# A gated SSM and MLP mix on one core: first tokens in two halves, PSUM seeds two tiles ahead, last output piece from another queue

## The chip, the cores and the metric

The kernel runs on one core of a Trainium2 chip. The metric is device time in microseconds of one execution. Most executions agree within 0.3%; one early execution of the kernel before took 283.59 us and is left out as not fast.

## The reference

For 2048 tokens of width 640, the result is a gated sum of a diagonal state-space model and a two-layer network. Cut to what matters:

```python
def reference(...):                                     # shortened
    g = sigmoid((x * gate_w).sum(-1, keepdims=True))
    # A: complex diagonal recurrence over the tokens
    Bu = einsum("bld,pd->blp", x, B_bar)                # B_bar, Lam_bar from Lambda, dt
    for t in range(L):
        h = Lam_bar * h + Bu[:, t, :]
    a = 2 * einsum("blp,dp->bld", hseq, Cmat).real + x * Dskip
    # B: two layers
    b = gelu(einsum("bsd,df->bsf", x, w1) + b1)
    b = einsum("bsf,fd->bsd", b, w2) + b2
    return g * a + (1 - g) * b
```

## The kernel before

The tokens go in four chunks of 512 (`CH`), each of four tiles of 128 (`P`). `ff1` is x·w1 with the gelu, `ssm` is x·B with the scan, `fin_b` is gelu·w2, `fin_a` is h·C plus the skip. TensorE does all the products, ScalarE (ACT) evacuates most of PSUM, into whose banks the products are written, and VectorE (DVE) does the complex rotations, the scans, and the last step of the output. In the traces DVE and ScalarE run their instructions in the order in which the program emits them (in the kernel before, DVE's L214, 216, 217, 218, 219, 221, 223 and 225 start in this order between 5.32 and 6.75 us).

The head. The first token chunk comes in two DMAs, then the first part of w1 in five strips (one per 128 rows, seven column tiles wide), all from one queue. TensorE warms up on zeros, transposes the tokens into five PSUM banks (one per 128 features), and starts `ff1`, strip by strip into seven banks:

```python
FA = KF // 2                       # 7 of 14 column tiles of w1 in the first strips
load_xn(0, 2)                      # tokens 0..255, then tokens 256..511
# ... parameters ...
for kd in range(KD):
    nc.sync.dma_start(out=w1a[kd][:], in_=B_w1[kd * P:(kd + 1) * P, 0:cut1])
# ... w1b, B, C, w2 ...
pTs = [bank(BF16) for _ in range(KD)]              # one PSUM bank per feature strip
for kd in range(KD):
    transposes(kd, 0)                              # tokens 0..255
nc.tensor.transpose(pA[:, 0:3 * KS], prmA[:], ident[0:3 * KS, 0:3 * KS])
for kd in range(KD):
    transposes(kd, 1)                              # tokens 256..511
# copies to SBUF: DVE takes strips 0, 2, 4 and ScalarE strips 1, 3
```

The seeds. The skip x·Dskip is not added at the end. DVE writes it into a PSUM bank first (`seed`), and the ten matmuls of `fin_a` accumulate onto it. The seed for a token tile is emitted one tile ahead:

```python
def fin_b(c):
    for a in range(TPC):
        if a == TPC - 1:
            seed(c * TPC)          # tile 0 of fin_a, one tile ahead
        # ... 28 matmuls, evacuated by ScalarE ...
def fin_a(c):
    for a in range(TPC):
        if a < TPC - 1:
            seed(ti + 1)
        # ... 20 matmuls onto the seeds, output step on DVE, DMA out ...
```

The planner. Where seeds, outputs and scan steps stand in DVE's order is decided while the program is built, by a small model of the engines' times. `pe(cols)` adds up TensorE's time from a starting value; a scan step is let out before a seed if the model says that it can start first. This number therefore changes the order of instructions and nothing else:

```python
class Clock:
    pe = 6.6
    act = 13.0
    dve = 0.0
```

## Time and profile before

| | kernel before |
|---|---|
| time, fast runs | 220.7 to 221.4 us |
| span of the profiled run | 219.2 us |
| TensorE, DVE, ScalarE busy | 97%, 86%, 43% |
| first `ff1` matmul (timeline) | 6.20 us |
| first matmul of `ssm(0)`, that is `BT_re` | 21.53 us |
| first matmul of `fin_a(0)`, that is `CT_re` | 73.47 us |
| last matmul starts, span ends | 216.07, 219.19 us |
| TensorE's waits for seeds (start to start) | 1.64 us |

Two lines of the page, the busy time of TensorE and the chain that ended last:

```profile
PE 213.4 (97%) x1276; PEld 125.1 (57%) x1287; DVE 189.3 (86%) x393; ACT 94.6 (43%) x153; POOL 5.0 (2%) x15
...
DVE 74%; PE 19%; issue 3%; DMA 2%; SPq 0%; DVEq 0%
```

TensorE is almost always busy, and yet the chain runs mostly through DVE. The two are as close as that: DVE is idle for only 2.9 us in all from 12.5 to 190 us, so a seed that stands late in DVE's order is late on the chip.

What TensorE waited for (name, then us in total, times, longest; the line of the start, before the first matmul, is left out):

```profile
...
PE bank L508 <- DVE bank L475: 0.7, 2, 0.5
PE bank L278 <- DMA w1a_80<-in_B_w_dram: 0.3, 1, 0.3
```

These totals count idle time from the modelled end of the last matmul, which lies after the moment when TensorE could have taken the next one. It is better to subtract starts. The timeline around 181 us (start, duration, engine, line, operation):

```profile
179.80 1.28 DVE L398 TENSOR_TENSOR_SCAN g<-r_c,carry,v 128x512 bf16<-128x512 f32 x1
180.32 0.84 PE L508 MATMUL bank<-CT_im,hs 128*128 128x320 bf16 x5
...
181.12 0.90 DVE L475 TENSOR_TENSOR bank<-xn,Dbc 128x320 f32<-128x320 bf16 x2
181.66 0.84 PE L508 MATMUL bank<-CT_re,hs 128*128 128x320 bf16 x5 [0.50 <-DVE bank L475]
```

Five matmuls of 320 columns are normally followed by the next five after 0.68 us. Here 181.66 − 180.32 = 1.34 us, so 0.66 us are lost (0.50 by the list of waits), while DVE finishes a scan and then writes the seed (181.12). Five such stretches (0.35 us at 79, 0.27 at 128, 0.18 at 131, 0.66 at 181, 0.18 at 184) add up to 1.64 us.

The head:

```profile
4.16 1.00 PE L197 MATMUL bank<-ident,xn 128*128 128x128 bf16 x10
...
5.21 0.73 PE L197 MATMUL bank<-ident,xn 128*128 128x128 bf16 x10
...
5.53 0.43 DVE L216 COPY xT_76<-bank 128x512 bf16<-128x512 bf16 x1
5.64 0.60 ACT L220 ACTIVATE xT_76<-bank 128x512 bf16<-128x512 bf16 x1
...
6.20 1.68 PE L278 MATMUL bank<-xT_76,w1a_80 128*128 128x512 bf16 x7 [0.25 <-DMA w1a_80<-in_B_w_dram]
...
11.12 0.31 ACT L263 ACTIVATE cq<-absq,halfpi 128x20 f32<-128x20 f32 x1
...
12.82 1.28 ACT L283 ACT_TABLE_LOAD   x1 [1.39 <-DVE colB L306]
...
14.12 1.26 ACT L283 ACTIVATE gel<-bank,colB 128x512 bf16<-128x512 f32 x2
```

The transposes of the second token half (`5.21`) run while TensorE has nothing else to do: the first weight strip lands at 6.15. Between the last of them and the first `ff1` matmul only 0.42 us are lost. DVE and ScalarE copy strips 0 and 1 at the same time (5.53 and 5.64), from two banks. ScalarE is done with the sines at 11.43, and its first gelu comes at 14.12.

The tail, the last five matmuls and the two issues that end the output:

```profile
215.85 0.44 PE L508 MATMUL bank<-CT_im,hs 128*128 128x128 bf16 x5
216.22 0.82 SPq L519 DMA_DIRECT2D out_dram<-ot  x2
```

The second of the two issues starts at 216.71 (the line merges both), 0.03 us after DVE has finished its data at 216.68.

### The profile page before, as it was taken

The page shows a single profiled execution, that of the slowest core. Times are in us where ns is not written, and L with a number is a line of the kernel's source. Part 1 is how long each engine was busy: PE and PEld are TensorE (multiplying, and loading weights), DVE is VectorE, ACT ScalarE, POOL GpSimd, SP SyncE. Part 2 cuts the span into 40 slices and gives each one's busy share as a digit, 9 for nine tenths or more (in the row PEclk, how much of TensorE's full clock was granted, in tenths as well). Part 3 has the DMA queues.
Part 4 walks back from the last instruction along what each step waited for, and adds up shares of the span by engine and source line. Part 5 has one row for each costly group of instructions (what it writes and reads, how often), then busy time and mean ns, then how long its engine had stood idle before and what let it go on. Part 6 is the DMA issues. An engine that isn't in the chain of part 4 may idle for free.

```text
span 219.2 us, 3326 instructions
## 1 busy us (share of the span) xinstructions
PE 213.4 (97%) x1276; PEld 125.1 (57%) x1287; DVE 189.3 (86%) x393; ACT 94.6 (43%) x153; POOL 5.0 (2%) x15
## 2 busy tenths in 40 slices
PE   7999999999999999999999999999999999999994
PEld 3444444444577765444467766444457776777773
DVE  1979999999999999999999999999999999800173
ACT  2779656675688102556652200456673210022100
POOL 6001000000000000000000000000000000000000
PEclk9999999999999999999999999999999999999999
DMA  6999999920000016000000003400000000200011
GB/s 192 355 229 171 224 290 300 197 87 0 0 0 3 0 42 201 0 0 0 0 3 0 0 3 92 147 1 3 0 0 0 3 0 30 71 22 1 0 64 60
DMA packets 31072, 15.31 MB, mean 70 GB/s; under 512 B 23823, under 2 KB 31056, under 8 KB 31056
## 3 DMA queue, kind: packets, MB, share of 16 engines
q1 hardware_dynamic: 30930, 15.09, 27.3%
q8 instruction: 10, 0.16, 0.3%
q14 instruction: 6, 0.05, 0.1%
q0 software_dynamic: 96, 0.00, 0.0%
q10 hardware_dynamic: 30, 0.00, 0.0%
HBM read 7.22 MB, written 2.62 MB: 45 GB/s over the span
## 4 chain that ended last, share of the span: by engine, by line
DVE 74%; PE 19%; issue 3%; DMA 2%; SPq 0%; DVEq 0%
DVE g L398 19%; DVE wb L379 11%; DVE wa L379 10%; PE bank L508 9%; PE bank L489 7%; DVE v L379 7%; DVE hs L379 6%; DVE ot L513 3%; DVE bank L475 3%; PE bank L278 3%; DMA w1a_80<-in_B_w_dram 2%; DVE CT_re L367 2%; DVE CT_im L367 2%; DVE g L329 1%; DVE TSIN L330 1%
## 5 line engine op out<-in xcount | busy, mean ns | idle before, releaser
L489 PE MATMUL bank<-w_sb,gel 128*128 128x320 bf16 x448 | 61.6, 299 | 0.0
L489 PEld LDWEIGHTS <-gel 128*128 128x128 bf16 x448 | 43.7, 98 | 17.7
L283 ACT ACTIVATE gel<-bank,colB 128x512 bf16<-128x512 f32 (+1 forms) x56 | 37.1, 694 | 16.8 <-PE bank L278 16.7
L445 ACT ACTIVATE bu<-bank 128x512 bf16<-128x512 f32 x40 | 23.9, 597 | 40.6 <-PE bank L442 28.6
L508 PEld LDWEIGHTS <-hs 128*128 128x128 bf16 x330 | 31.8, 98 | 13.5 <-issue 1.8
L398 DVE TENSOR_TENSOR_SCAN g<-r_c,carry,v 128x512 bf16<-128x512 f32 x30 | 37.1, 1269 | 0.0
L492 ACT ACTIVATE gb<-bank,gcol 128x320 f32<-128x320 f32 x32 | 16.4, 528 | 46.2 <-PE bank L489 46.2
L508 PE MATMUL bank<-CT_re,hs 128*128 128x320 bf16 (+2 forms) x165 | 27.1, 295 | 0.8 <-DVE bank L475 0.7
L513 DVE SCALAR_TENSOR_TENSOR ot<-bank,gcol,gb 128x320 bf16<-128x320 f32 (+2 forms) x33 | 17.6, 534 | 11.9 <-PE bank L508 11.7
L508 PE MATMUL bank<-CT_im,hs 128*128 128x320 bf16 (+2 forms) x165 | 27.1, 295 | 0.0
L475 DVE TENSOR_TENSOR bank<-xn,Dbc 128x320 f32<-128x320 bf16 (+2 forms) x33 | 14.4, 481 | 6.3 <-ACT gb L492 6.3
L442 PEld LDWEIGHTS <-BT_im 128*128 128x128 bf16 x100 | 9.8, 98 | 11.8
L442 PEld LDWEIGHTS <-BT_re 128*128 128x128 bf16 x100 | 9.8, 98 | 11.5
L379 DVE TENSOR_TENSOR v<-wa,wb 128x512 bf16<-128x512 bf16 x40 | 15.2, 421 | 0.6
L379 DVE TENSOR_TENSOR wa<-TCOS,g 128x1024 bf16<-128x1024 bf16 x20 | 13.7, 685 | 0.1
L379 DVE TENSOR_TENSOR wa<-TCOS,bu 128x1024 bf16<-128x1024 bf16 x20 | 13.7, 684 | 0.0
L379 DVE TENSOR_TENSOR wb<-TSIN,g 128x1024 bf16<-128x1024 bf16 x20 | 13.7, 683 | 0.0
L379 DVE TENSOR_TENSOR wb<-TSIN,bu 128x1024 bf16<-128x1024 bf16 x20 | 13.7, 683 | 0.0
L398 DVE TENSOR_TENSOR_SCAN g<-r_c,v 128x512 bf16<-128x512 f32 x10 | 11.7, 1208 | 0.0
L379 DVE TENSOR_TENSOR hs<-wa,wb 128x512 bf16<-128x512 bf16 x20 | 8.5, 423 | 0.6
L379 DVE TENSOR_TENSOR hs<-wb,wa 128x512 bf16<-128x512 bf16 x20 | 8.4, 418 | 0.0
L442 PE MATMUL bank<-xT_76,BT_im 128*128 128x512 bf16 x25 | 6.2, 379 | 0.0
(157 smaller groups left out, 242.0 us busy)
## 6 DMA issues: line engine op xcount, KB each, us to landing
out_dram<-ot SPq DMA_DIRECT2D x15, 160.0 KB, 1.8
w_sb<-in_B_w_dram SPq DMA_DIRECT2D x1, 2080.0 KB
xn<-in_A_x_dram SPq DMA_DIRECT2D x3, 640.0 KB, 5.1
xn<-in_A_x_dram SPq DMA_DIRECT2D x2, 320.0 KB, 3.4
gz<-zrow SPq DMA_DIRECT2D x16, 0.5 KB, 2.0
w1a_80<-in_B_w_dram SPq DMA_DIRECT2D x1, 224.0 KB, 4.4
w1a_81<-in_B_w_dram SPq DMA_DIRECT2D x1, 224.0 KB
w1a_82<-in_B_w_dram SPq DMA_DIRECT2D x1, 224.0 KB, 4.6
```

The source lines that it names most:

```text
L278: nc.tensor.matmul(p[:m, :], lhsT=w, rhs=xT[c][:, kd, :], start=(kd == 0), stop=(kd == KD - 1))
L283: nc.scalar.activation(out=gel[c][:m, kf, :], in_=p[:m, :], func=ACT.Gelu_apprx_tanh, bias=b1_c[:m, kf:kf + 1])
L367: nc.vector.scalar_tensor_tensor(out=CT[:, ks, :], in0=CT[:, ks, :], scalar=sc[:, ks:ks + 1], in1=t[:], op0=ALU.mult, op1=ALU.add)
L379: nc.vector.tensor_tensor(out=o, in0=a, in1=b, op=op)
L398: nc.vector.tensor_tensor_scan(s["g"][:, ri, :], r_c[:, ks:ks + 1].to_broadcast([P, CH]), s["v"][:, ri, :], init, ALU.mult, ALU.add)
L442: nc.tensor.matmul(p[:], lhsT=BT[:, kd, ks * P:(ks + 1) * P], rhs=xT[c][:, kd, :], start=(kd == 0), stop=(kd == KD - 1))
L445: nc.scalar.activation(out=bu[:, ri, :], in_=p[:], func=ACT.Identity)
L475: dve_now(ck.pe, 0.45, lambda: nc.vector.tensor_tensor(out=p[:, 0:d1 - d0], in0=xn[c][:, a, d0:d1], in1=Dbc[:, d0:d1], op=ALU.mult))
L489: nc.tensor.matmul(p[:, 0:d1 - d0], lhsT=gel[c][:m, kf, lo:lo + P], rhs=w2_sb[:m, kf, d0:d1], start=(kf == 0), stop=(kf == KF - 1))
L492: nc.scalar.activation(out=gb[:, d0:d1], in_=p[:, 0:d1 - d0], func=ACT.Identity, scale=gcol[:, 1, ti:ti + 1])
L508: nc.tensor.matmul(p[:, 0:d1 - d0], lhsT=hs[c][:, j, lo:lo + P], rhs=CT[:, j % KS, d0:d1], start=False, stop=(j == 2 * KS - 1), skip_group ...
L513: nc.vector.scalar_tensor_tensor(out=ot[:, d0:d1], in0=p[:, 0:d1 - d0], scalar=gcol[:, 0, ti:ti + 1], in1=gbs[ti][:, d0:d1], op0=ALU.mult, ...
```

## The change

The intent, in three parts: start `ff1` on the first 256 tokens as soon as their tokens and the first weight strip are there, with the other 256 tokens loaded behind the strips; emit each seed two tiles ahead; and send the last 32 KB of output from ScalarE's queue so that it does not queue behind the piece before. The planner's starting number changes too, from 6.6 to 5.2, as the head is to start earlier. The warm-up on zeros is shortened as well, from seven matmuls of 512 columns to six and two of 128; it belongs to the head. Cut to its core:

```diff
-FA = KF // 2
+FA = 6
-    load_xn(0, 2)
+    load_xn(0, 0, H)
     for kd in range(KD):
         nc.sync.dma_start(out=w1a[kd][:], in_=B_w1[kd * P:(kd + 1) * P, 0:cut1])
+    load_xn(0, H, TPC)
 # ...
-        pe = 6.6
+        pe = 5.2
 # ...
-    pTs = [bank(BF16) for _ in range(KD)]
+    pT = bank(BF16)
+    def strip(kd, h):            # strips 0..3 share one bank, strip 4 lies in pA's
+        return pT[:, kd * HT:(kd + 1) * HT] if kd < 4 else pA[:, (h + 1) * HT:(h + 2) * HT]
+    def take(kd, h):
+        dst = xT[0][:, kd, h * HT:(h + 1) * HT]
+        if kd % 2 == 0:
+            nc.vector.tensor_copy(out=dst, in_=strip(kd, h))
+        else:
+            nc.scalar.activation(out=dst, in_=strip(kd, h), func=ACT.Identity)
 # ... first-half transposes and take(kd, 0), then colA and the first trigonometry steps
+    for kd in range(KD):
+        if kd == KD - 1:
+            transposes(1)
+            for j in range(KD):
+                take(j, 1)
+        for kf in range(FA):
+            ff1_mm(banks[kf], 0, kf, kd, 0, HT)
 # ... the sines; then the same 30 matmuls for the second half, and the gelus
-            if a == TPC - 1:
-                seed(c * TPC)
+            if a >= TPC - 2:
+                seed(c * TPC + a - (TPC - 2))
-            if a < TPC - 1:
-                seed(ti + 1)
+            if a < TPC - 2:
+                seed(ti + 2)
 # ...
-                    nc.sync.dma_start(out=out2d[ti * P:(ti + 1) * P, s0:d1], in_=ot[:, s0:d1])
+                    q = nc.sync if i == 1 else nc.scalar
+                    q.dma_start(out=out2d[ti * P:(ti + 1) * P, s0:d1], in_=ot[:, s0:d1])
```

Below, "the head" is the first part with all that belongs to it, "the seeds" and "the tail" are the other two, and "the planner's number" is the 5.2.

More of the change, by code (lines that the diff above doesn't have):

```diff
@@ L110, with load_xn @@
     H = TPC // 2
-    def load_xn(c, parts=1):
-        xn[c] = xnp.tile([P, TPC, D], BF16, name="xn")
-        n = TPC // parts
-        for h in range(parts):
-            r0 = c * CH + h * n * P
-            nc.sync.dma_start(out=xn[c][:, h * n:(h + 1) * n, :], in_=x2d[r0:r0 + n * P, :].rearrange("(a p) d -> p a d", p=P))
-    load_xn(0, 2)
+    def load_xn(c, a0=0, a1=TPC):
+        if a0 == 0:
+            xn[c] = xnp.tile([P, TPC, D], BF16, name="xn")
+        r0 = c * CH + a0 * P
+        nc.sync.dma_start(out=xn[c][:, a0:a1, :], in_=x2d[r0:r0 + (a1 - a0) * P, :].rearrange("(a p) d -> p a d", p=P))
+    load_xn(0, 0, H)
     nc.scalar.dma_start(out=prmA[0:KS, :], in_=A_log_dt.rearrange("(j p) -> j p", p=P))
@@ L189, with transposes @@
     wps = bank()
-    for _ in range(7):
+    for _ in range(6):
         nc.tensor.matmul(wps[:], lhsT=warm[:, 0:P], rhs=warm[:], start=True, stop=True)
+    for _ in range(2):
+        nc.tensor.matmul(wps[:, 0:P], lhsT=warm[:, 0:P], rhs=warm[:, 0:P], start=True, stop=True)
     pA = bank(BF16)
-    pTs = [bank(BF16) for _ in range(KD)]
-    def transposes(kd, h):
-        for a in range(h * H, (h + 1) * H):
-            nc.tensor.transpose(pTs[kd][:, a * P:(a + 1) * P], xn[0][:, a, kd * P:(kd + 1) * P], ident[:])
-    for kd in range(KD):
-        transposes(kd, 0)
+    pT = bank(BF16)
+    HT = H * P
+    def strip(kd, h):
+        return pT[:, kd * HT:(kd + 1) * HT] if kd < 4 else pA[:, (h + 1) * HT:(h + 2) * HT]
+    def transposes(h):
+        for kd in range(KD):
+            o = strip(kd, h)
+            for a in range(H):
+                nc.tensor.transpose(o[:, a * P:(a + 1) * P], xn[0][:, h * H + a, kd * P:(kd + 1) * P], ident[:])
+    def take(kd, h):
[4 more added lines that the diff above has]
+            nc.scalar.activation(out=dst, in_=strip(kd, h), func=ACT.Identity)
+    transposes(0)
     nc.tensor.transpose(pA[:, 0:3 * KS], prmA[:], ident[0:3 * KS, 0:3 * KS])
-    for kd in range(KD):
-        transposes(kd, 1)
     def col(name, dtype=F32, n=KS):
@@ L213 @@
     r_c = col("r_c")
+    for kd in range(KD):
+        take(kd, 0)
     nc.vector.tensor_copy(out=colA[:], in_=pA[:, 0:3 * KS])
     nc.scalar.activation(out=dt16[:], in_=ldt_c, func=ACT.Exp)
-    nc.vector.tensor_copy(out=xT[0][:, 0, :], in_=pTs[0][:, 0:CH])
     nc.vector.tensor_copy(out=dt32[:], in_=dt16[:])
@@ L219 @@
     nc.vector.tensor_tensor(out=th_c[:], in0=dt32[:], in1=lim_c, op=ALU.mult)
-    nc.scalar.activation(out=xT[0][:, 1, :], in_=pTs[1][:, 0:CH], func=ACT.Identity)
     nc.vector.tensor_scalar(out=thp_c[:], in0=th_c[:], scalar1=INV_2PI, scalar2=None, op0=ALU.mult)
     nc.scalar.activation(out=r_c[:], in_=dtl[:], func=ACT.Exp)
-    nc.vector.tensor_copy(out=xT[0][:, 2, :], in_=pTs[2][:, 0:CH])
-    nc.scalar.activation(out=xT[0][:, 3, :], in_=pTs[3][:, 0:CH], func=ACT.Identity)
-    nc.vector.tensor_copy(out=xT[0][:, 4, :], in_=pTs[4][:, 0:CH])
     scr = gelp.tile([P, KF * CH // 2], F32, name="gel")
@@ L253, with ff1_mm, ff1_act, ff1 @@
     nc.vector.tensor_tensor(out=red, in0=u, in1=kk[:], op=ALU.subtract)
+    sth, cth = sq[:, 0:KS], cq[:, 0:KS]
+    sL, cL = sq[:, KS:2 * KS], cq[:, KS:2 * KS]
+    sH, cH = sq[:, 2 * KS:3 * KS], cq[:, 2 * KS:3 * KS]
+    sQ, cQ = sq[:, 3 * KS:4 * KS], cq[:, 3 * KS:4 * KS]
+    hs = [None] * NCH
+    gel = [None] * NCH
+    gbs = [None] * NT
+    sizes = [P] * (KF - 1) + [F_LAST + 1]
+    def ff1_mm(p, c, kf, kd, t0=0, t1=CH):
+        m = sizes[kf]
+        w = w1a[kd][:, kf * P:kf * P + m] if kf < FA else w1b[kd][:, (kf - FA) * P:(kf - FA) * P + m]
+        nc.tensor.matmul(p[:m, t0:t1], lhsT=w, rhs=xT[c][:, kd, t0:t1], start=(kd == 0), stop=(kd == KD - 1))
+        pe(t1 - t0)
+    def ff1_act(p, c, kf):
+        m = min(sizes[kf], F - kf * P)
+        nc.scalar.activation(out=gel[c][:m, kf, :], in_=p[:m, :], func=ACT.Gelu_apprx_tanh, bias=b1_c[:m, kf:kf + 1])
+        act(0.69)
+        if kf == KF - 1:
+            nc.scalar.activation(out=zrow[F_LAST:F_LAST + 1, :], in_=p[F_LAST:F_LAST + 1, :], func=ACT.Tanh, scale=0.5)
+            act(0.6)
+            for a in range(TPC):
+                ti = c * TPC + a
+                nc.sync.dma_start(out=gz[:, ti:ti + 1], in_=zrow[F_LAST:F_LAST + 1, a * P:(a + 1) * P])
+    def ff1(c, k0=0):
+        for kf in range(k0, KF):
+            p = bank()
+            for kd in range(KD):
+                ff1_mm(p, c, kf, kd)
+            ff1_act(p, c, kf)
+            let_out(ck.pe)
+    def gel_tile(c):
+        gel[c] = gelp.tile([P, KF, CH], BF16, name="gel")
+        nc.gpsimd.memset(gel[c][F_LAST:F_LAST + 1, KF - 1, :], 1.0)
+    gel_tile(0)
+    banks = [bank() for _ in range(FA)]
+    for kd in range(KD):
+        if kd == KD - 1:
[4 more added lines that the diff above has]
+            ff1_mm(banks[kf], 0, kf, kd, 0, HT)
     nc.scalar.activation(out=FS[:, :, 0:HC], in_=red, func=ACT.Sin, scale=TWO_PI_M)
@@ L263 @@
     nc.scalar.activation(out=cq[:], in_=absq[:], func=ACT.Sin, scale=-TWO_PI_M, bias=halfpi[:])
-    sth, cth = sq[:, 0:KS], cq[:, 0:KS]
-    sL, cL = sq[:, KS:2 * KS], cq[:, KS:2 * KS]
-    sH, cH = sq[:, 2 * KS:3 * KS], cq[:, 2 * KS:3 * KS]
-    sQ, cQ = sq[:, 3 * KS:4 * KS], cq[:, 3 * KS:4 * KS]
-    hs = [None] * NCH
-    gel = [None] * NCH
-    gbs = [None] * NT
-    sizes = [P] * (KF - 1) + [F_LAST + 1]
-    def ff1_mm(p, c, kf, kd):
-        m = sizes[kf]
-        w = w1a[kd][:, kf * P:kf * P + m] if kf < FA else w1b[kd][:, (kf - FA) * P:(kf - FA) * P + m]
-        nc.tensor.matmul(p[:m, :], lhsT=w, rhs=xT[c][:, kd, :], start=(kd == 0), stop=(kd == KD - 1))
-        pe(CH)
@@ L281, in ff1_act @@
-    def ff1_act(p, c, kf):
-        m = min(sizes[kf], F - kf * P)
-        nc.scalar.activation(out=gel[c][:m, kf, :], in_=p[:m, :], func=ACT.Gelu_apprx_tanh, bias=b1_c[:m, kf:kf + 1])
-        act(0.69)
-        if kf == KF - 1:
-            nc.scalar.activation(out=zrow[F_LAST:F_LAST + 1, :], in_=p[F_LAST:F_LAST + 1, :], func=ACT.Tanh, scale=0.5)
-            act(0.6)
-            for a in range(TPC):
-                ti = c * TPC + a
-                nc.sync.dma_start(out=gz[:, ti:ti + 1], in_=zrow[F_LAST:F_LAST + 1, a * P:(a + 1) * P])
@@ L292, in ff1 @@
-    def ff1(c):
-        gel[c] = gelp.tile([P, KF, CH], BF16, name="gel")
-        nc.gpsimd.memset(gel[c][F_LAST:F_LAST + 1, KF - 1, :], 1.0)
-        groups = [range(0, FA)] if c == 0 else []
-        groups += [[kf] for kf in range(FA if c == 0 else 0, KF)]
-        for kfs in groups:
-            banks = {}
-            for kd in range(KD):
-                for kf in kfs:
-                    if kd == 0:
-                        banks[kf] = bank()
-                    ff1_mm(banks[kf], c, kf, kd)
-                if c == 0 and kfs[0] == 0 and kd == 3:
-                    nc.tensor.transpose(pA[:, P:P + NB], prmB[:], ident[0:NB, 0:NB])
-                    nc.vector.tensor_copy(out=colB[:], in_=pA[:, P:P + NB])
-                    for j in range(KD):
-                        nc.vector.tensor_copy(out=w1b[j][:, n1b - 1:n1b], in_=pA[:, P + j:P + j + 1])
-            for kf in kfs:
-                ff1_act(banks[kf], c, kf)
-            let_out(ck.pe)
@@ L313 @@
-    ff1(0)
+    for kd in range(KD):
+        for kf in range(FA):
+            ff1_mm(banks[kf], 0, kf, kd, HT, CH)
+        if kd == 2:
+            nc.tensor.transpose(pA[:, P:P + NB], prmB[:], ident[0:NB, 0:NB])
+            nc.vector.tensor_copy(out=colB[:], in_=pA[:, P:P + NB])
+            for j in range(KD):
+                nc.vector.tensor_copy(out=w1b[j][:, n1b - 1:n1b], in_=pA[:, P + j:P + j + 1])
+    for kf in range(FA):
+        ff1_act(banks[kf], 0, kf)
+    ff1(0, FA)
     lo, hi = slice(0, HC), slice(HC, HB)
@@ L523 @@
     ssm(0)
+    gel_tile(1)
     ff1(1)
@@ L533 @@
     ssm(2)
+    gel_tile(2)
     ff1(2)
@@ L539 @@
     ssm(3)
+    gel_tile(3)
     ff1(3)
```

## The prediction

> **What bounds it now.** The page gives TensorE 213.4 of 219.2 us (97%) at full granted clock. From its first FF1 matmul (6.20 us, timeline) to the last one (216.3) it issues matmul after matmul: 216 ns per 512 columns, 136 ns per 320. DVE is busy 86% and has almost no idle from 12.5 to 190 us, so it is the near-critical second engine; the chain of waits running through DVE (74%) reflects that it is always late, not that TensorE starves: the list of waits charges DVE with only 0.7 us of TensorE idle. Start-to-start distances say more: five stretched steps in the output matmuls (L508), all waiting for a PSUM skip seed (L475): 0.35 us at 79, 0.27 at 128, 0.18 at 131, 0.66 at 181, 0.18 at 184: 1.64 us. The head costs 6.2 us: transposes 4.16 to 5.9, then about 0.3 us for the first weight strip, landed at 6.15 (DMA issues). The tail after the last matmul is 2.9 us.
>
> **What changes.**
> 1. Seeds two tiles ahead. No work added (16 tiles either way). In the new DVE order each seed stands one tile earlier. Walking that order with the trace's durations (seed pair 0.80 us, scan 1.19, wide product 0.60, output 0.45 us of DVE time) every seed is done 2 us or more before its matmul; hs of chunk 0 moves behind four seeds, to about 72.5, needed after 73.7. Gain: nearly all of 1.64 us, on the critical path since TensorE is dense elsewhere.
> 2. Head. The DMA engines are full from 2.5 us (350 to 400 GB/s by windows). The first strip now has 328+197 KB in front of and in it, before 655+229: 360 KB less at about 350 GB/s, so landing at 5.1 instead of 6.15. First half transposes end about 5.1. So FF1 starts near 5.2 instead of 6.2. But ten second-half transposes, formerly run inside that wait, now stand in the FF1 stream: 10 x 58 ns = 0.58 us. The second token half, now queued behind five strips, lands near 8.0 (estimate from w1a_84's 8.47 and 163 KB less); TensorE reaches it at 5.2 + 4 x 6 x 109 ns = 7.8: 0.1 to 0.3 us of new wait. Thirty extra matmuls cost 30 x 2.5 ns = 0.08 us (the Trainium skill, "TensorE: Matmul & The Clock Gate", "Wait — 56ns, not 53.3ns?", gives N/2.4 GHz + 2.5 ns; the trace's 216 ns at 512 agrees). Net gain about 0.3 us, not 1. The trigonometry on DVE starts about 0.6 us earlier (12.3 instead of 12.98), more slack for everything on DVE.
> 3. Last piece from ScalarE's queue. The SyncE queue issued it at 216.71, 0.03 us after its data (216.68): nothing to win. The Trainium skill, "DMA: Bandwidth & Descriptors", "Issuing engines are not separate DMA queues", says a second issuer saves only issue time. 0 +- 0.15 us.
>
> **Time.** Fast runs of before: 220.8 to 221.3, profile 221.0. Minus 1.6, minus 0.3: 219.1 to 219.2 us, 0.8% less: inside 2%. Range 218.3 to 220.4. Faster by over 2%: 2%; within: 97%; slower: 1%.
>
> **What the profile would show.** No TensorE wait for DVE seeds in L529 (step 1 right). First FF1 matmul 5.1 to 5.4, the w1a_0 landing about 5.1; a TensorE gap of 0.1 to 0.3 us before the second transposes; first BT_re matmul at 21.2 instead of 21.53 (step 2 right). The distance from last matmul to end still 2.8 to 3.0 us (step 3).
>
> **What would make it wrong.** The second token half landing after 8.5 us, which eats the head's gain; DVE reaching the second half's copies late, behind the trigonometry (about 8.6, needed 9.3); seeds that wait for a PSUM bank and stall DVE in order; output evictions late enough to hold banks from the next matmuls.

## The result and the profile after

The changed kernel took 220.37 us (median of 6 runs, 219.99 to 220.39) against 221.23 us (median of the five fast runs). A ratio here is the mean time of one kernel's fast runs over that of the other's of the same rounds, so not quite the ratio of the medians. It is 0.9965, with a 95% interval from 0.995 to 0.998: 0.35% or 0.8 us less, where 0.8% or 1.9 us had been predicted.

| | before | after | predicted |
|---|---|---|---|
| first `ff1` matmul | 6.20 | 5.39 | 5.1 to 5.4 |
| first `w1` strip landed | 6.15 | 4.42 | 5.1 |
| second token half landed | 4.79 | 8.33 | 8.0 |
| first gelu | 14.12 | 15.29 | not given |
| first matmul of `ssm(0)` | 21.53 | 22.50 | 21.2 |
| first of `fin_a(0)` to last matmul | 142.60 | 140.98 | about 141.0 (142.60 less 1.6) |
| last matmul's start to end of span | 3.12 | 3.17 | unchanged |
| waits for seeds | 1.64 | 0 | nearly 0 |

The stages from 73 us on did what was predicted; the head went 0.97 us the wrong way. The same lines of the page:

```profile
PE 213.6 (98%) x1318; PEld 128.3 (59%) x1318; DVE 189.7 (87%) x396; ACT 94.6 (43%) x155; POOL 4.9 (2%) x15
...
PE 93%; ACT 3%; DVE 2%; issue 0%
```

The chain no longer runs through DVE. TensorE's waits, again without the start:

```profile
...
PE bank L278 <- ACT gel L283: 0.4, 1, 0.4
PE bank L206 <- DMA xn<-in_A_x_dram: 0.2, 1, 0.2
PE bank L278 <- DVE xT_76 L211: 0.2, 1, 0.2
```

No seed is left in this list, and three waits of the head have come. Around 181 us:

```profile
176.78 0.88 DVE L496 TENSOR_TENSOR bank<-xn,Dbc 128x320 f32<-128x320 bf16 x2
...
179.70 0.90 DVE L496 TENSOR_TENSOR bank<-xn,Dbc 128x320 f32<-128x320 bf16 x2
...
180.50 0.84 PE L529 MATMUL bank<-CT_im,hs 128*128 128x320 bf16 x5
...
181.18 0.84 PE L529 MATMUL bank<-CT_re,hs 128*128 128x320 bf16 x5
```

The starts of TensorE stand 0.68 us apart. The seed of the tile that waited before, the second of `fin_a(2)`, is written at 176.78 and done 3.5 us before its first matmul (181.18); what DVE writes at 179.70 is the seed of the third tile. The head:

```profile
5.05 0.29 DVE L211 COPY xT_76<-bank 128x256 bf16<-128x256 bf16 x1 [3.51 <-PE bank L206]
...
5.37 0.39 ACT L213 ACTIVATE xT_76<-bank 128x256 bf16<-128x256 bf16 x1 [2.09 <-DVE xT_76 L211]
5.39 0.82 PE L278 MATMUL bank<-xT_76,w1a_80 128*128 128x256 bf16 x6 [0.16 <-DVE xT_76 L211]
5.79 0.49 DVE L211 COPY xT_76<-bank 128x256 bf16<-128x256 bf16 x2 [0.45 <-ACT xT_76 L213]
...
6.12 0.38 ACT L213 ACTIVATE xT_76<-bank 128x256 bf16<-128x256 bf16 x1 [0.36 <-DVE xT_76 L211]
...
7.35 0.82 PE L278 MATMUL bank<-xT_76,w1a_83 128*128 128x256 bf16 x6
...
8.38 0.73 PE L206 MATMUL bank<-ident,xn 128*128 128x128 bf16 x10 [0.20 <-DMA xn<-in_A_x_dram]
...
8.71 0.83 DVE L263 TENSOR_TENSOR gel<-gel,bu 128x640 f32<-128x640 f32 x1
...
9.45 0.28 DVE L211 COPY xT_76<-bank 128x256 bf16<-128x256 bf16 x1
...
9.79 0.81 PE L278 MATMUL bank<-xT_76,w1a_80 128*128 128x256 bf16 x6
...
10.51 0.38 ACT L213 ACTIVATE xT_76<-bank 128x256 bf16<-128x256 bf16 x1 [0.36 <-DVE xT_76 L211]
...
10.91 1.28 ACT L314 ACT_TABLE_LOAD   x1
...
13.68 0.30 ACT L323 ACTIVATE cq<-absq,halfpi 128x20 f32<-128x20 f32 x1
...
13.99 1.28 ACT L283 ACT_TABLE_LOAD   x1
...
15.22 0.38 PE L278 MATMUL bank<-xT_76,w1b_89 128*128 128x512 bf16 x1
...
16.03 0.38 PE L278 MATMUL bank<-xT_76,w1b_85 128*128 128x512 bf16 x1 [0.42 <-ACT gel L283]
```

Read it in five places. (1) The copies of a half go hand over hand: DVE 5.05, ScalarE 5.37, DVE 5.79, ScalarE 6.12. (2) TensorE comes to the second half at 8.01 us (7.35 plus six steps of 0.109) and takes its first transpose at 8.38. (3) Its last transpose starts at 8.89, but the first copy follows only at 9.45, because DVE is in the third step of the trigonometry (from 8.71). In late_transposes below, where DVE was idle, the first copy starts 0.15 us after the last transpose's start (9.30 and 9.45). So here the copies came some 0.4 us after their bank was ready, and an earlier landing alone would not have moved them: that is an estimate from these times. (4) The second half's copies end at 10.89, and only then does ScalarE load its table for the sines; its sines end at 13.98, and the gelu's table is there at 15.27. (5) After 15.22 TensorE's next matmul comes at 16.03 instead of 15.44: it needs a PSUM bank that the first gelu must free. The tail, with the last issue on ScalarE's queue:

```profile
215.19 0.44 PE L529 MATMUL bank<-CT_im,hs 128*128 128x128 bf16 x5
...
216.06 0.38 ACTq L541 DMA_DIRECT2D out_dram<-ot  x1
```

The head's 0.97 us, worked out from start-to-start distances in the two timelines: the first `ff1` matmul 0.81 us earlier; ten transposes of 56 ns in the stream, +0.56; wait for the second half, +0.37; wait for its copies at 9.49, +0.19; wait for the gelu, +0.59; 30 more matmuls at about 2 ns, +0.07. The sum is +0.97.

### The profile page after: what moved, and what is told of

Same layout as the page of the kernel before. It is cut to its first block, busy times and chain, and to the rows that moved or that the text cites. A ratio compares the mean times of both kernels' runs of the same rounds, so it can differ in the third digit from the quotient of the medians.

```text
span 218.6 us, 3401 instructions
## 1 busy us (share of the span) xinstructions
PE 213.6 (98%) x1318; PEld 128.3 (59%) x1318; DVE 189.7 (87%) x396; ACT 94.6 (43%) x155; POOL 4.9 (2%) x15
## 4 chain that ended last, share of the span: by engine, by line
PE 93%; ACT 3%; DVE 2%; issue 0%
PE bank L510 28%; PE bank L278 24%; PE bank L529 20%; PE bank L463 20%; PE bank L191 1%; ACT xT_76 L213 1%; ACT L283 1%; ACT L314 1%; DVE xT_76 L211 1%; PE bank L206 0%; DVE gel L261 0%; DVE gel L263 0%; ACT hs L316 0%; ACT gel L283 0%; DVE bu L262 0%
## 5 line engine op out<-in xcount | busy, mean ns | idle before, releaser
L463 PE MATMUL bank<-xT_76,BT_re 128*128 128x512 bf16 x25 | 6.2, 379 | 0.0
```

The lines of the kernel that those rows point to most:

```text
L463: nc.tensor.matmul(p[:], lhsT=BT[:, kd, ks * P:(ks + 1) * P], rhs=xT[c][:, kd, :], start=(kd == 0), stop=(kd == KD - 1))
```

## The experiments

All give correct results. Each is timed in 5 rounds against the kernel before (two_banks in 3). Times from here on are medians.

| run | us | ratio to before, 95% | first `ff1` | `ssm(0)` | seed waits | full speed from |
|---|---|---|---|---|---|---|
| after | 220.37 | 0.9965 (0.995 to 0.998) | 5.39 | 22.50 | 0 | 4.8 |
| seeds_only | 219.13 | 0.9913 (0.9899 to 0.9926) | 6.07 | 21.41 | 0 | 4.9 |
| head_only | 220.89 | 0.9987 (0.9974 to 1.0) | 5.39 | 22.49 | 0.59 | 6.2 |
| tail_only | 221.43 | 1.0005 (0.9992 to 1.0019) | 6.24 | 21.58 | 1.61 | 5.3 |
| two_banks | 219.98 | 0.9943 (0.993 to 0.9956) | 5.60 | 22.20 | 0 | 7.0 |
| clock_only | 220.01 | 0.9942 (0.9929 to 0.9956) | 6.38 | 21.73 | 0.46 | 5.7 |
| head_old_clock | 222.16 | 1.0041 (1.0027 to 1.0054) | 5.39 | 22.61 | 1.83 | 7.2 |
| dve_copies | 220.03 | 0.9937 (0.9921 to 0.9953) | 5.39 | 22.21 | 0 | 7.0 |
| late_transposes | 220.39 | 0.9962 (0.9949 to 0.9976) | 4.96 | 22.50 | 0 | 4.0 |
| seeds_and_clock | 219.49 | 0.9931 (0.9919 to 0.9944) | 6.29 | 21.64 | 0 | 5.5 |
| fixed_head | 219.61 | 0.9935 (0.9923 to 0.9948) | 5.39 | 21.66 | 0 | before 5.4 |
| seeds_fa6 | 219.32 | 0.9921 (0.9908 to 0.9935) | 6.40 | 21.74 | 0 | 6.1 |

The last column is when matmul starts, 107 ns apart at 128 columns (about 214 at 256), close up to 56 (109). It differs from profile to profile though the first matmul always starts at 1.20, so a head is to be compared across profiles with that column in sight. In the profile of the kernel before it is 4.7, so a later full speed, from the shorter warm-up or otherwise, does not explain the 0.97 us between that profile and the one after (4.8).

### seeds_only: the seeds alone

The kernel before, and nothing but this:

```diff
-            if a == TPC - 1:
-                seed(c * TPC)
+            if a >= TPC - 2:
+                seed(c * TPC + a - (TPC - 2))
-            if a < TPC - 1:
-                seed(ti + 1)
+            if a < TPC - 2:
+                seed(ti + 2)
```

> Only the seeds two tiles ahead, head and tail of before. Theory A (seed step was right, head step wrong): the 1.64 us of TensorE waits for seeds disappear and nothing replaces them: about 219.6 us, 0.7% less than before; first BT_re matmul stays at 21.5. Theory B (the seeds stopped waiting in the changed kernel only because its head was 1 us late): waits of 0.5 us or more remain in the output matmuls and the gain is under 1 us (220.3 or more).

Measured: 219.13 us, ratio 0.9913. No TensorE wait for a seed is left; from the first of `fin_a(0)` (73.35) to the last matmul (214.33) it takes 140.98 us, to the hundredth what the changed kernel takes. Theory A held and B fell. This kernel beats both; its interval and that of the changed kernel do not meet.

### head_only: the head alone, with its planner's number

The changed kernel with the seeds and the tail of before:

```diff
-            if a >= TPC - 2:
-                seed(c * TPC + a - (TPC - 2))
+            if a == TPC - 1:
+                seed(c * TPC)
-            if a < TPC - 2:
-                seed(ti + 2)
+            if a < TPC - 1:
+                seed(ti + 1)
-                    q = nc.sync if i == 1 else nc.scalar
+                    q = nc.sync
```

> Only the two-half head; seeds and tail of before. Theory A: first BT_re matmul at 22.5 as in the changed kernel (1.0 us later than before), seed waits still about 1.6 us, so about 222.2 us, 0.4% slower than before. Theory B: head about neutral (220.9 to 221.4), because it gives back its loss through shorter seed waits.

Measured: 220.89 us, ratio 0.9987. The time is B's, but half of A stands too: `ssm(0)` starts at 22.49, 0.96 us late. The seed waits fell from 1.64 to 0.59 us and paid for it. Why they fell was open. The scans had not moved against TensorE: the trigonometry's second stage starts at 14.00 instead of 12.98, as late as TensorE. That left DVE's order, which the planner's number decides.

### tail_only: the last piece from ScalarE's queue alone

```diff
-                    nc.sync.dma_start(out=out2d[...], in_=ot[:, s0:d1])
+                    q = nc.sync if i == 1 else nc.scalar
+                    q.dma_start(out=out2d[...], in_=ot[:, s0:d1])
```

> Only the last piece from the ScalarE queue. My theory: 0 +- 0.1 us, distance from the last matmul's start to the end 3.1 us as before (3.12). Rival (the change's intent): 0.2 us or more shorter.

Measured: ratio 1.0005, and 3.17 us from the last matmul's start to the end, against 3.12. The expectation held: nothing gained. The Trainium skill, "DMA: Bandwidth & Descriptors", section "Issuing engines are not separate DMA queues", says that a second issuer saves only the time to issue. Here the queue of before was free 0.03 us after the data, so there was none to save.

### two_banks: no shared bank for the copies

```diff
-        return pT[:, kd * HT:(kd + 1) * HT] if kd < 4 else pA[:, (h + 1) * HT:(h + 2) * HT]
+        return (pT if kd % 2 == 0 else pA)[:, (kd // 2 + kd % 2) * HT:(kd // 2 + kd % 2 + 1) * HT]
```

> The changed kernel with even strips of the transposes in one PSUM tile (copied by DVE) and odd ones in the other (copied by ScalarE), so that copies of the two engines no longer wait for each other. Theory C (the alternation on one PSUM tile delays the copies, then ScalarE's sines and the first gelu): second-half copies end near 10.2 instead of 10.9, first gelu at about 14.6 instead of 15.3, wait of 0.59 us at 15.2 falls below 0.15, 219.7 us. Theory D (the second half's landing at 8.33 and the trigonometry alone make the gelu late): wait stays at 0.45 or more, time within 0.2 us of the changed kernel.

Measured: 219.98 us; first gelu 14.55; no wait for it. The first copies in this kernel's timeline:

```profile
5.26 0.69 DVE L211 COPY xT<-bank 128x256 bf16<-128x256 bf16 x3 [3.57 <-PE bank L206]
...
5.38 0.66 ACT L213 ACTIVATE xT<-bank 128x256 bf16<-128x256 bf16 x2 [2.10 <-PE bank L216]
5.60 1.56 PE L278 MATMUL bank<-xT,w1a 128*128 128x256 bf16 x7 [0.26 <-DVE xT L211]
```

Three DVE copies and two of ScalarE now overlap and end at 6.04 instead of 6.50. They start later, at 5.26 instead of 5.05; ScalarE's wait ends with the transpose of the parameters (L216, at 5.16), which shares the bank of the odd strips, and why DVE waits as long was not tested. In the second half ScalarE's copies end at 10.17 instead of 10.89. Theory C held: the alternation on one bank is what made ScalarE late. The Trainium skill says why the program must alternate: "PSUM — Partial Sum Buffer", section "PSUM bank collisions raise a hardware error", tells that two engines on one bank and quadrant at once are a collision, two readers included, so accesses have to be ordered by bank. The timelines agree: overlap from two banks, hand over hand from one. `ssm(0)` still starts at 22.20, not near 21.9: in this profile the array ran at half speed until 7.0 us, so the first seven `ff1` matmuls took 1.40 us instead of 0.76.

### clock_only: the planner's number alone

```diff
-        pe = 6.6
+        pe = 5.2
```

> The kernel before with one number changed: the planner's starting time of TensorE, 5.2 instead of 6.6 us, which decides where seeds and outputs stand among the scan work in DVE's order. Theory E (this number, not any shift of DVE against TensorE, gave back the head's loss in head_only): seed waits fall from 1.64 to about 0.6 us with the head unchanged (first BT_re at 21.5), so about 220.1 us, 0.5% less. Rival F (the waits fell because the head changed when things happen): waits stay at 1.3 us or more and the time within 0.2 us of before.

Measured: 220.01 us, ratio 0.9942, seed waits 0.46 us in place of 1.64. Two waits of the list became one:

```profile
PE bank L508 <- DVE bank L475: 0.3, 1, 0.3
```

Theory E held, F fell. No work and no load was changed: DVE runs the same instructions in another order, with seeds earlier among the scan steps.

### head_old_clock: the head alone, with the old number

head_only with

```diff
-        pe = 5.2
+        pe = 6.6
```

> The two-half head alone, with the planner's number put back to 6.6. Theory E: the head's loss shows whole: first BT_re at 22.3 to 22.6, seed waits back at 1.4 us or more, about 222.0 us, 0.4% slower than before. Rival F: as head_only, 220.9 us.

Measured: 222.16 us, ratio 1.0041. The seed waits are 1.83 us:

```profile
PE bank L529 <- DVE bank L496: 1.2, 2, 0.6
```

With its number taken away, the head shows its cost: 0.9 us. That includes seed waits 0.19 us longer than before. E held again.

### dve_copies: all ten half copies on DVE

```diff
-        if kd % 2 == 0:
-            nc.vector.tensor_copy(out=dst, in_=strip(kd, h))
-        else:
-            nc.scalar.activation(out=dst, in_=strip(kd, h), func=ACT.Identity)
+        nc.vector.tensor_copy(out=dst, in_=strip(kd, h))
```

> The changed kernel with all ten half-strip copies on DVE. Theory C (the copies alternate between DVE and ScalarE on one PSUM tile and wait for each other; then ScalarE, in order, starts its sines late and the first gelu is late): ScalarE is free, first gelu at about 14.0 instead of 15.3, no wait at the third single FF1 group (0.59 us in the changed kernel), 219.8 us. Rival (DVE alone is no faster and the trigonometry is as late): first gelu at 15 or later, 220.3 us.

Measured: 220.03 us. ScalarE's timeline in this kernel:

```profile
7.11 1.28 ACT L311 ACT_TABLE_LOAD   x1
...
12.30 0.31 ACT L320 ACTIVATE cq<-absq,halfpi 128x20 f32<-128x20 f32 x1
12.62 1.28 ACT L280 ACT_TABLE_LOAD   x1
13.92 2.42 ACT L280 ACTIVATE gel<-bank,colB 128x512 bf16<-128x512 f32 x4
```

The sines' table is loaded at 7.11 instead of 10.91 and the first gelu comes at 13.92 instead of 15.29; the 0.59 us wait is gone. With two_banks, a second way of freeing ScalarE, this settles the cause of the gelu wait. What is left of the loss in this profile is the second half, which landed at 8.81, and the late full speed (7.0).

### late_transposes: fill the wait for the second half

The changed kernel with

```diff
-        if kd == KD - 1:
-            transposes(1)
-            for j in range(KD):
-                take(j, 1)
         for kf in range(FA):
             ff1_mm(banks[kf], 0, kf, kd, 0, HT)
+        if kd == KD - 1:
+            transposes(1)
+            for j in range(KD):
+                take(j, 1)
```

> The changed kernel with the second-half transposes after the fifth strip's first-half matmuls instead of before them. The wait for the second token half (0.37 us) is filled by six matmuls; the copies then are later by some 0.2 us, so the wait for them grows from 0.19 to about 0.4 and the late gelu stays. Expect 0.2 us less at the first single FF1 group (13.1 instead of 13.28) and nothing at the first BT_re (22.4 to 22.6), since the gelu decides: 220.2 to 220.4 us. If the landing decides instead, BT_re comes 0.3 us earlier and the time is 220.0.

Measured: 220.39 us. `ssm(0)` starts at 22.50, as expected, and the wait for the copies is 0.43 us. But the first single group starts at 13.28, not 13.1. In this run the second half landed at 8.70 and the second strip at 6.12, where TensorE lost 0.56 us. Its timeline after the landing:

```profile
8.80 0.72 PE L206 MATMUL bank<-ident,xn 128*128 128x128 bf16 x10
9.79 0.38 PE L278 MATMUL bank<-xT,w1a 128*128 128x256 bf16 x2 [0.27 <-DVE xT L211]
```

So the gelu decides, as expected, and the 0.2 us that I expected before it were not there to be seen.

### seeds_and_clock: do the two cures add up?

seeds_only with

```diff
-        pe = 6.6
+        pe = 5.2
```

> The head and tail of before, seeds two tiles ahead, and the planner's number 5.2. Theory E (the number and the seeds two ahead are two cures of the same seed waits): no seed waits, as in seeds_only, so the same time, 219.1 to 219.4 us. Rival (their gains of 1.9 and 1.2 us add up): 218.2 us or less.

Measured: 219.49 us, ratio 0.9931; no seed waits. The time is 0.09 us above the range that was expected, but far from the rival's 218.2. They do not add up: the seeds two ahead alone clear all 1.64 us, and the number then has nothing to do.

### fixed_head: the head with its three waits taken out

dve_copies, with the second token half loaded after the second strip, its transposes and copies behind the matmuls of the second strip:

```diff
     for kd in range(KD):
+        if kd == 2:
+            load_xn(0, H, TPC)
         nc.sync.dma_start(out=w1a[kd][:], ...)
-    load_xn(0, H, TPC)
 # ...
-        if kd == KD - 1:
+        if kd == 2:
             transposes(1)
             for j in range(KD):
                 take(j, 1)
+            # u, kk, red: the first three trigonometry steps, moved here
```

> The changed kernel with all half-strip copies on DVE, the second token half loaded after the second weight strip instead of after the fifth, its transposes and copies after the second strip's matmuls, and the trigonometry's first three DVE steps behind those copies. Theory G (even without its waits the two-half head has almost nothing to win, because the ten transposes that ran in the DMA wait now stand in the dense stream): no wait of 0.2 us or more between first FF1 matmul and first BT_re; first BT_re at 21.3 to 21.5 if the array speeds up before 5.5 us, up to 22.1 if later; time 219.0 to 219.6, equal to seeds_only within noise. Rival H (the two-half head done right is worth its 0.8 us): 218.6 or less.

Measured: 219.61 us, ratio 0.9935. TensorE in the head of this kernel:

```profile
5.39 1.47 PE L273 MATMUL bank<-xT,w1a 128*128 128x256 bf16 x12
7.00 0.73 PE L207 MATMUL bank<-ident,xn 128*128 128x128 bf16 x10
...
13.03 1.24 PE L273 MATMUL bank<-xT,w1b 128*128 128x512 bf16 x5
```

`ssm(0)` starts at 21.66. The full-speed condition was met and I had expected 21.5 at most; one wait of 0.31 us, for the second half at 6.58, remained where I had expected none of 0.2. The time, at the upper end of G's range, is still G's: about 0.7 us better than the changed kernel, no better than seeds_only (0.9913), and far from H's 218.6. Even without this wait `ssm(0)` would start at 21.35, against 21.41 in seeds_only.

### seeds_fa6: narrower first strips with the old head

seeds_only with

```diff
-FA = KF // 2
+FA = 6
```

> seeds_only with first weight strips of six column tiles (192 KB) instead of seven (224 KB): the first strip should land about 0.1 us earlier, so the first FF1 matmul at 5.9 to 6.05 instead of 6.07: 219.0 to 219.2 us, at most 0.1% less than seeds_only. If it is slower than seeds_only by 0.2 us or more, the earlier group end brings a PSUM or weight wait.

Measured: 219.32 us, ratio 0.9921, the same as seeds_only within the intervals. The first strip did land earlier (5.62 against 5.79), but in this profile half speed lasted until 6.1 and `ff1` began at 6.40, held up by the transposes. Whether the narrower strip gains 0.1 us stays open; it is below what these runs tell.

## Why the prediction was wrong

The direction was right, the size was not: 0.8 us less in place of 1.9. The final time of 220.37 us lay at the very edge of the range.

- **Seeds: right.** Predicted nearly all of 1.64 us. The waits are gone, and the stretch from `fin_a(0)` on is 1.62 us shorter. seeds_only took 1.9 us off (0.9913 of 221.15), of which 0.12 us is a head that happened to run earlier in the profile.
- **Tail: right.** Predicted 0 ± 0.15 us; measured nothing.
- **Head: wrong, and this is the step that failed.** The prediction said "Net gain about 0.3 us"; the chip gave a loss of 0.97 us in the profile and 0.9 us in head_old_clock. Its terms: start at 5.39 instead of 5.2 (0.19 us): the transposes ended near 5.1 as predicted and the strip was there at 4.42, but the first copy, 0.29 us long, starts only at 5.05, after the tenth transpose has started (4.90), and the prediction had no time for it; transposes in the stream 0.56 us, as predicted (0.58); the second half landed at 8.33 instead of 8.0 (8.18 to 8.86 in the five other runs with this order of loads), a wait of 0.37 us against the predicted 0.1 to 0.3; and two terms that the sum did not have, the wait for the copies (0.19 us) and for the first gelu (0.59 us).
- **Why those two were missing.** The prediction named the first as a risk, but had DVE free of the trigonometry by "about 8.6"; its third step only started at 8.71, and the copy behind it came at 9.45. As for the gelu, I walked DVE's order and not ScalarE's. I said that "the trigonometry on DVE starts about 0.6 us earlier (12.3 instead of 12.98)"; it started at 14.01. In the changed program ScalarE's half copies stand before its sines, they alternate with DVE's on one bank, and those of the second half came only after the landing (8.33) and behind DVE's trigonometry (first copy 9.45). The runs two_banks and dve_copies each take the alternation away and each remove the gelu wait. The order of instructions was to be seen before the run, and so was the shared bank in the diff.
- **Why the landing was late.** I took the landing of the last strip of before, 8.47, and subtracted 163 KB at the "350 to 400 GB/s" of the prediction; its own windows showed less from 4.0 to 5.5 us (324, 268 and 287). In the window from 2 to 8.5 us the DMAs moved 332 GB/s before and 316 after (290 to 317 in the five other kernels that load the second half behind the strips). The loads are now cut into narrower rows (1536 instead of 1792 bytes), but no run changed the width alone with this order, so that cause is not shown. It has evidence against it: in the old order of loads the narrow rows moved 345 GB/s (seeds_fa6) and the wide ones 343 (seeds_only). The cause stays open. By the estimate above, the late landing did not decide in the profile after, where the copies stood behind the trigonometry anyway.
- **What I did not see at all: the planner's number.** It was in the diff and worth 1.25 us by itself (clock_only, 0.9942), as a second cure of the same seed waits. It made head_only look neutral. In the whole change it gains nothing, since the seeds have already cleared the waits.

The account by runs: seeds −1.9, head without its number +0.9, tail 0, together −1.0 us, against −0.8 measured; each term has an interval of about ±0.3.

What stays open: how much of the head's loss in any one run is due to the array's late full speed. The old head spends much of that time on transposes and in a DMA wait; the new one fills it with `ff1`. In the profiles of two_banks, dve_copies and head_old_clock seven or eight `ff1` matmuls ran at half speed, some 0.7 us of array time. In dve_copies and head_old_clock the late landing (8.81 and 8.86) would have made TensorE wait anyway; in two_banks (8.18) it would not, so part of that time was lost there. How the loss of the changed kernel divides between the trigonometry, the landing and the shared bank is also open: fixed_head changes all three at once.

## What to carry to other kernels

An earlier start is worth only what the work moved out of its shade leaves of it: ten transposes that ran free in a DMA wait cost 0.56 us once they stood in a dense stream, and of 0.81 us of earlier start only 0.18 could have been kept (0.81 − 0.56 − 0.07). Before moving work between engines, walk the order of every engine that will wait for it, and look for PSUM banks that two engines share. When a change sets a planning number as well, undo it by itself: here it hid the loss of one part behind the gain of another.

## What the Trainium skill lacked or had wrong

- "TensorE: Matmul & The Clock Gate", "What's actually happening", gives a transition to full speed that varies by ±500 ns. The spread here is larger: full speed came between 4.0 and 7.2 us in thirteen profiles whose first matmul all started at 1.20, and at 4.8, 6.2 and 7.2 in three whose heads are alike (after, head_only, head_old_clock). A note in the same section, by which one kernel had 6, 11 or 14 slow matmuls, is closer to that.
- The same page, "Back-to-back issue gap", gives a sustained spacing of 81 ns at 128 columns and 131 ns at 512 for streams of weight load and matmul. Here such streams ran at 56 ns and 216 ns, and at 109 ns for 256: its formula N/2.4 + 2.5 holds, its sustained figures do not.
- "ScalarE: Activation LUTs", "What ACT_TABLE_LOAD costs", gives 2.66 us for a switch of tables, drain included. In dve_copies the last sine ends at 12.61 and the first gelu starts at 13.92, with a load of 1.28 us between: 1.31 us.
- "PSUM — Partial Sum Buffer" states the rule that two engines must not be on one bank at once; no page gives what obeying it costs. Here the copies of the first half, taken in turn from one bank, ended 0.46 us later (6.50 and 6.04) than from two banks, where the first of them started 0.21 us later (5.05 and 5.26).
